# The head of a fused attention and MLP kernel: no entry barrier, eight warm matmuls instead of ten, one copy moved from VectorE to ScalarE

## The chip, the cores and the metric

The kernel runs on one core of one Trainium2 chip. The metric is the device time of one execution in microseconds (us), here the median of several runs. Each run also has a span, from the first to the last of the program's own instructions, which is 1.2 to 1.4 us shorter than the time in most runs. The granted clock is the share of TensorE's full clock that the profile records. PE is TensorE, DVE is VectorE, ACT is ScalarE, POOL is GpSimd, SP is SyncE.

## The reference

The input x has 2048 tokens of 448 values (bfloat16). It is layer-normalised and goes through two branches: a linear attention with 16 heads, and an MLP with squared ReLU. The result is `x + attention * silu(mlp)`.

```python
xn = _layernorm(x, axis=-1)
s = _A_ref(xn, A_wqkv, A_wo)                       # linear attention, then @ wo
g = _silu(_B_ref(xn, B_w1, B_b1, B_w2, B_b2))      # relu(xn @ w1 + b1)**2 @ w2 + b2
return x + s * g
```

Only the first 10 us matter here. In them the first four tiles of 128 tokens are loaded, normalised, transposed on PE, copied from PSUM to SBUF and multiplied with the first weights.

## The kernel before

The kernel records every operation with what it reads and writes. A list scheduler fixes the order on each engine, and each engine then runs its list strictly in order, with semaphore waits. The parts that the change touches (cuts are marked):

```python
# loads: which queue issues them, and in what order
table = add("act", lambda e, _: e.preload_act_table_set("natural_log_exp_and_others"), [], ["actw"], 0.1)
table.prio = -120
load_x(0, 1)                                        # x of tile 0, SP's queue
load_x(1, 2, "act", ["ones"]).prio = -118           # x of tile 1, ACT's queue, after POOL's memset of "ones"
twins = load_k("sp", w_qkv, A_wqkv, "wk", 384, 2 * D, later=True)   # key weights, SP's queue
load_x(2, 4)
# ... (cut)
# layer norm of a tile: statistics on DVE (bn_stats, bn_aggr), Ln and Exp on ACT, normalise on DVE
# ... (cut)
def warm(n, wide=False, after=()):                  # matmuls on constant data
    # ... (cut)
warm(10, wide=True)
# ... (cut)
# the order of the head on DVE and ACT, fixed by hand
("dve", "st0 mv0 st1 mv1 xn00 xn01 xd0 xn10 xn11 xd1 st2 mv2 xT11 st3 mv3 xn2 xd2 xn3 xd3 xT3"),
("act", "ln0 ex0 ln1 ex1 xT00 xT01 xT10 ln2 ex2 b1 ln3 ex3 xT2"),
```

The digit after a name is the tile: `st` and `mv` are its statistics, `ln` and `ex` Ln and Exp, `xn` the normalise, `xd` a small copy beside it, `xT` the copy of the transposed tile out of PSUM. Nothing uses the results of the warm matmuls; they keep PE busy until the first real work. In the profile of this kernel matmuls of 512 columns start 0.427 us apart until about 6.7 us (the slow rate) and 0.216 us apart afterwards (the fast rate).

## Time and profile before

| | before |
|---|---|
| time, median of the first 3 runs | 142.06 us (142.0 to 142.11) |
| span of the profiled run (another one, of 142.56 us) | 141.3 us |
| PE busy | 137.9 us, 98% of the span |
| matmuls back to back from | 9.86 us to the end |
| first transposes on PE | 5.06 us |

These are lines of the page of the kernel before: the busy times with the share of the span, and the chain of work that ended last, followed back from the end.

```profile
PE 137.9 (98%) x1225; PEld 68.3 (48%) x1225; DVE 92.2 (65%) x224; ACT 78.6 (56%) x152; POOL 22.9 (16%) x38
...
PE 98%; DVE 0%; issue 0%; DVEq 0%
```

The kernel is bound by PE. After 9.86 us PE has work without a break, so whatever moves the end has to move the start of this dense stretch, or put a stall into it.

The next lines are from the timeline of the kernel before: its first 7.4 us, and the line with which the dense stretch begins. The columns are start and duration in us, engine, line, operation, what is written from what, and how many; in brackets stands the idle time of the engine before it and what ended it. A DMA line shows the issue alone, not the transfer.

```profile
0.80 0.39 SPq L396 DMA_DIRECT2D x_tok<-in_A_x_dram  x1
...
0.84 4.42 PE L1042 MATMUL pb<-const-bfloat16-1.0 128*128 128x512 bf16 x10 [0.84 <-PEq L1210]
...
0.93 0.40 ACTq L396 DMA_DIRECT2D x_tok<-in_A_x_dram  x1
...
1.25 0.42 SPq L396 DMA_DIRECT2D w_qkv<-in_A_wqkv_dram  x1
...
3.17 0.63 DVE L458 BATCH_NORM_STATS2 st<-x_tok 128x6 f32<-128x448 bf16 x1 [3.17 <-DMA x_tok<-in_A_x_dram]
...
3.93 0.59 DVE L458 BATCH_NORM_STATS2 st<-x_tok 128x6 f32<-128x448 bf16 x1
...
4.66 0.55 DVE L481 TENSOR_SCALAR xn<-x_tok,mv,rstd 128x256 bf16<-128x256 bf16 x2
...
5.06 1.08 PE L510 MATMUL pb<-ident,xn 128*128 128x128 bf16 x6
...
9.86 0.39 PE L621 MATMUL pb<-w_qkv,xT 64*128 64x512 bf16 x2
```

No DMA and no matmul starts before 0.80, because all engines wait for the entry barrier; only POOL's four memsets of constants come earlier, from 0.30.

### The profile page before, as it was taken

How to read it: one execution, taken by the hardware profiler on the slowest of the kernel's cores; microseconds unless marked ns; L12 is line 12 of the kernel's file. 1: busy time of each engine (PE TensorE's matmuls, PEld its weight loads, DVE VectorE, ACT ScalarE, POOL GpSimd, SP SyncE). 2: the span in 40 equal slices, each digit the busy share in tenths (PEclk: the TensorE clock that was granted, in tenths of full speed). 3: DMA queues.
4: the chain of work that ended last, by engine and by line, in shares of the span. 5: the costliest groups of instructions: out<-in, count | busy, mean ns of one | idle time of the engine just before them, and what ended most of it. 6: DMA issues, size and time to landing. Idle time of an engine off the chain costs nothing.

```text
span 141.3 us, 3056 instructions
## 1 busy us (share of the span) xinstructions
PE 137.9 (98%) x1225; PEld 68.3 (48%) x1225; DVE 92.2 (65%) x224; ACT 78.6 (56%) x152; POOL 22.9 (16%) x38
## 2 busy tenths in 40 slices
PE   7999999999999999999999999999999999999992
PEld 2366444444444444444455445644555555555482
DVE  1989978898878997779959910226956062452753
ACT  3658787987888897879799561333033030300220
POOL 6000000000000000000670000000001419092670
DMA  4989266999813400000000026991000202122032
GB/s 117 296 288 264 52 167 115 365 300 195 140 24 70 84 14 0 0 15 8 0 0 0 5 80 148 180 167 21 5 0 0 69 1 89 41 67 68 32 100 69
DMA packets 20210, 12.91 MB, mean 91 GB/s; under 512 B 9380, under 2 KB 19812, under 8 KB 20196
## 3 DMA queue, kind: packets, MB, share of 16 engines
q1 hardware_dynamic: 18188, 11.45, 32.9%
q10 hardware_dynamic: 2008, 1.27, 4.2%
q8 instruction: 10, 0.16, 0.5%
q14 instruction: 4, 0.03, 0.1%
HBM read 8.78 MB, written 2.10 MB: 77 GB/s over the span
## 4 chain that ended last, share of the span: by engine, by line
PE 98%; DVE 0%; issue 0%; DVEq 0%
PE pb L935 30%; PE pb L668 30%; PE pb L621 9%; PE pb L1001 8%; PE pb L702 7%; PE pb L652 6%; PE pb L1042 3%; PE pb L510 1%; PE pb L708 1%; PE pb L795 1%; PE pb L756 1%; PE pb L833 0%; DVE xn L971 0%; PE pb L826 0%; DVE xn L980 0%; PE pb L791 0%
## 5 line engine op out<-in xcount | busy, mean ns | idle before, releaser
L668 PE MATMUL pb<-xT,w 64*128 64x512 bf16 (+2 forms) x408 | 51.3, 365 | 0.0
L935 PE MATMUL pb<-w,r 64*128 64x448 bf16 (+3 forms) x378 | 44.9, 343 | 0.0
L677 ACT ACTIVATE r<-pb,b1f 128x512 bf16<-128x512 f32 x56 | 34.9, 689 | 2.8 <-PE pb L668 2.8
L668 PEld LDWEIGHTS pb<-xT,w 64*128 64x128 bf16 (+1 forms) x408 | 22.8, 94 | 22.1 <-ACT r L677 0.5
L935 PEld LDWEIGHTS pb<-w,r 64*128 64x128 bf16 (+1 forms) x378 | 22.7, 95 | 20.3 <-issue 0.7
L911 ACT ACTIVATE gbuf<-gbuf 128x448 bf16<-128x448 bf16 (+1 forms) x16 | 8.6, 564 | 36.7 <-DVE gbuf L946 34.5
L946 DVE TENSOR_TENSOR gbuf<-pb,b2b 128x448 bf16<-128x448 f32 (+1 forms) x16 | 9.3, 608 | 28.9 <-PE pb L935 28.9
L980 POOL TENSOR_TENSOR xn<-xn,x_tok 128x448 bf16<-128x448 bf16 x15 | 15.0, 1031 | 48.9 <-DVE xn L971 48.9
L621 PE MATMUL pb<-w_qkv,xT 64*128 64x512 bf16 (+1 forms) x106 | 18.0, 380 | 0.0
L652 PE MATMUL pb<-xT,w_qkv 64*128 64x512 bf16 x84 | 15.5, 376 | 0.0
L685 DVE TENSOR_TENSOR r<-r 128x512 bf16<-128x512 bf16 x39 | 13.5, 418 | 0.0
L385 POOL MEMSET kvm<- 128x2048 bf16 x1 | 1.8, 1804 | 64.3 <-DVE zb L646 64.3
L458 DVE BATCH_NORM_STATS2 st<-x_tok 128x6 f32<-128x448 bf16 x16 | 9.3, 612 | 3.6 <-DMA x_tok<-in_A_x_dram 3.6
L609 DVE SCALAR_TENSOR_TENSOR qk<-pb,qk 128x512 bf16<-128x512 f32 x16 | 10.7, 686 | 0.3
L599 ACT ACTIVATE qk<-pb 128x512 bf16<-128x512 f32 x16 | 8.9, 595 | 3.6 <-PE pb L621 3.0
L1001 PE MATMUL pb<-msb,pqT 64*128 64x448 bf16 (+3 forms) x93 | 10.9, 343 | 0.0
L971 DVE TENSOR_TENSOR xn<-pb,gbuf 128x448 bf16<-128x448 f32 (+2 forms) x17 | 9.2, 591 | 2.0 <-ACT gbuf L911 1.5
L686 ACT ACTIVATE r<-r 128x512 bf16<-128x512 bf16 x17 | 9.7, 650 | 0.0
L621 PEld LDWEIGHTS pb<-w_qkv,xT 64*128 64x128 bf16 (+1 forms) x106 | 6.6, 94 | 6.2 <-DVE xT L520 0.2
L702 PE MATMUL pb<-qk,xn 128*128 128x448 bf16 x48 | 9.4, 352 | 0.0
L599 ACT ACTIVATE pqT<-pb 128x512 bf16<-128x512 f32 x12 | 6.8, 597 | 3.2 <-PE pb L668 1.6
L652 PEld LDWEIGHTS pb<-xT,w_qkv 64*128 64x128 bf16 x84 | 6.0, 94 | 5.0
(77 smaller groups left out, 98.9 us busy)
## 6 DMA issues: line engine op xcount, KB each, us to landing
out_dram<-xn SPq DMA_DIRECT2D x15, 112.0 KB, 1.7
w<-in_B_w_dram SPq DMA_DIRECT2D x1, 1568.0 KB, 9.9
x_tok<-in_A_x_dram SPq DMA_DIRECT2D x3, 448.0 KB, 3.8
xT<-rows ACTq DMA_DIRECT2D x6, 112.0 KB
w<-in_B_w_dram SPq DMA_DIRECT2D x1, 576.0 KB, 5.6
xT<-rows SPq DMA_DIRECT2D x5, 112.0 KB
w_o<-in_A_wo_dram SPq DMA_DIRECT2D x1, 392.0 KB, 11.2
w_qkv<-in_A_wqkv_dram SPq DMA_DIRECT2D x1, 384.0 KB, 3.4
```

Of the source, the lines that this page charges most:

```text
L599: add("act", lambda e, _: e.activation(out=slot, in_=src(), func=AF.Exp), [buf, "actw"], [tile], 0.6)
L609: lambda e, _: e.scalar_tensor_tensor(out=slot, in0=src(), scalar=1.0 + 1e-6, in1=slot, op0=ALU.add, op1=ALU.max),
L621: return e.matmul(ps(b)[:, 0:512], xT[half[h], c, si * P : (si + 1) * P], w_qkv[half[h], c, 384 : 2 * D], start=start, stop=stop,)
L652: return e.matmul(ps(b)[:, 0:512], w_qkv[half[h], c, m * P : (m + 1) * P], xT[half[h], c, g * 512 : (g + 1) * 512], start=start, stop=stop,)
L668: return e.matmul(ps(b)[:, c0 : c0 + n], w_1[half[h], c, fi * P : (fi + 1) * P], xT[half[h], c, t : t + n], start=start, stop=stop,)
L677: lambda e, _: e.activation(out=slot, in_=ps(b)[:, 0:512], func=AF.Relu, bias=b1f[:, fi : fi + 1]),
L685: return e.tensor_tensor(out=slot, in0=slot, in1=slot, op=ALU.mult)
L686: return e.activation(out=slot, in_=slot, func=AF.Square)
L702: last = e.matmul(ps(b)[:, 0:D], xn[:, si, c * P : (c + 1) * P], pk_of(si), start=(si == 0), stop=(si == NT - 1),)
L935: return e.matmul(ps(b)[:, 0:n], r2[half[h], fi, si * P : (si + 1) * P], w_2[half[h], fi, c], start=start, stop=stop)
L980: eng, lambda e, _: e.tensor_tensor(out=ob, in0=ob, in1=x_tok[:, si, c], op=ALU.add),
L1001: return e.matmul(ps(b)[:, 0:n], q, m, start=start, stop=stop)
```

## The change

The intent is to start earlier. The entry instructions that the program builder (Bacc) puts in front of the kernel (a drain and a barrier on each engine, four memsets of constants) are filtered out. The warm matmuls, which read one of those constants, now read the kernel's own `ones`, a constant that POOL writes first. There are eight of them, since PE starts earlier. ACT instead of DVE copies the second half of tile 1's transpose, so that DVE can take tile 3's statistics at once. And the load of tile 1 on ACT's queue, which waited for `ones`, now waits for `eps5`, POOL's second memset.

```diff
+    entry = nc.main_func.blocks[0].instructions
+    entry[:] = [i for i in entry if i.opcode not in ("Drain", "EventSemaphore", "Memset")]
 ... (cut)
-        pool(lambda e, _: e.memset(b1r[:, :], 0.0), ["b1r"], dur=0.2)
-        junk = nc.const_aps.tensor(1.0, [P, 512], bf)
+        junk = bass.AP(tensor=ones[:, :].tensor, offset=ones[:, :].offset, ap=[ones[:, :].ap[0], [0, 512]])
+        pool(lambda e, _: e.memset(ones[:, :], 1.0), ["ones"], dur=0.1).prio = -130
+        pool(lambda e, _: e.memset(eps5[:, :], 1e-5), ["eps5"], dur=0.1).prio = -129
+        pool(lambda e, _: e.memset(b1r[:, :], 0.0), ["b1r"], dur=0.2).prio = -128
 ... (cut: the old memsets of eps5 and ones go)
-        load_x(1, 2, "act", ["ones"]).prio = -118
+        load_x(1, 2, "act", ["eps5"]).prio = -118
 ... (cut)
-            add("pe", f, list(after), [b], n * (0.426 if wide else 0.107))
-        warm(10, wide=True)
+            add("pe", f, ["ones", *after], [b], n * (0.426 if wide else 0.107))
+        warm(8, wide=True)
 ... (cut)
-        turn(1, 1, "dve")
+        turn(1, 1, "act")
 ... (cut)
-            ("dve", "st0 mv0 st1 mv1 xn00 xn01 xd0 xn10 xn11 xd1 st2 mv2 xT11 st3 mv3 xn2 xd2 xn3 xd3 xT3"),
-            ("act", "ln0 ex0 ln1 ex1 xT00 xT01 xT10 ln2 ex2 b1 ln3 ex3 xT2"),
+            ("dve", "st0 mv0 st1 mv1 xn00 xn01 xd0 xn10 xn11 xd1 st2 mv2 st3 mv3 xn2 xd2 xn3 xd3 xT3"),
+            ("act", "ln0 ex0 ln1 ex1 xT00 xT01 xT10 xT11 ln2 ex2 b1 ln3 ex3 xT2"),
```

More of the change, by code (lines that the diff above doesn't have):

```diff
@@ L356, in bass_recurrent_scan__linear_attn_block__dense_activation_squared_relu__prompt_kernel @@
         )
-        pool(lambda e, _: e.memset(eps5[:, :], 1e-5), ["eps5"], dur=0.1)
         def keep(name, view, pattern, base, cm):
@@ L373, in bass_recurrent_scan__linear_attn_block__dense_activation_squared_relu__prompt_kernel @@
         pool(lambda e, _: e.memset(eps6[:, :], 1e-6), ["eps6"], dur=0.1)
-        pool(lambda e, _: e.memset(ones[:, :], 1.0), ["ones"], dur=0.1)
         qk_of = lambda si: qk[:, si // 2, :].rearrange("p (j t c) -> p t j c", t=2, c=64)[:, si % 2]
```

## The prediction

> **What bounds it now.** The page gives PE 137.9 of a 141.3 us span, and the chain that ended last is PE for 98% of it. From 9.86 us to the end the timeline shows matmuls back to back. So the end time is the moment at which the dense stretch begins (9.86 us) plus a nearly fixed 131.4 us.
>
> The head, from the timeline: entry barrier until 0.73 us; first x load issued 0.80, statistics of tile 0 start 3.17 when it lands; ten warm matmuls 0.84 to 5.06, 0.427 us apart; first transposes at 5.06, released by DVE's normalised tile at 5.03, so the warm matmuls end just as their successor becomes ready. DVE is then busy 80 to 97% to 9 us. Matmuls run at the slow rate until about 6.70 (starts 0.427 us apart), then 0.216 us apart.
>
> **What the change does.**
> 1. Entry barrier gone. SP ran its drain at 0.0, so x of tile 0 can be issued at about 0.05 instead of 0.80: the whole DVE chain (statistics, normalise, transposes) moves up about 0.7 us. POOL's first memset stays at 0.30, so PE, which needs "ones", starts near 0.47, only 0.37 us earlier.
> 2. Eight warm matmuls: 0.47 + 8 x 0.427 = 3.9; the transposes are ready at about 4.3. PE idles some 0.4 us.
> 3. Clock. The fast rate came 5.9 us after the first matmul. The Trainium skill, "TensorE: Matmul & The Clock Gate", Part 1, says the window is about 3.4 us and free-running; the 5.9 us fits one partly filled window and a full one. If the switch moves with PE's start (0.37 us) or stays, 0.35 to 0.75 us of the first key matmuls run at half rate: 0.2 to 0.35 us of the 0.7 handed back.
> 4. xT of tile 1, second half, to ACT. DVE loses a 0.29 us copy and 0.16 us of wait, so tile 3 statistics start about 0.46 us earlier. But ACT does the copy (0.35 us) before the Ln/Exp of tile 2, which were at 6.93 and 7.25 while PE's transposes for this copy ended near 7.0: rstd of tile 2 comes about 0.45 later and tile 2's normalise hardly moves (8.02 before, relative to the chain). Tile 3's Ln stands behind the b1 copy on ACT, which waits for PE, so its normalise (8.70) does not move either. Worth 0 to 0.1 us.
>
> Sum: 0.7 - 0.2 (clock) + 0.05, about 0.55 us at the start of the dense stretch, all on the critical path, since PE is dense afterwards. The list schedule is recomputed; I allow 0.2 us either way for rearranged evictions later.
>
> **Predicted: 141.5 us, range 141.05 to 141.95.** Faster by over 2%: 0.01; within 2%: 0.98; slower: 0.01.
>
> **What would show it.** First x issue at 0.0 to 0.1 and first statistics near 2.4 to 2.5; first warm matmul 0.4 to 0.5, the eighth over by 3.9; a gap of PE of about 0.4 us; first transposes near 4.3; the fast rate from 6.3 to 6.7 at latest, so that the first key matmuls show 0.427 us; DVE idle about 0.4 us before tile 2's normalise; dense stretch from about 9.3; from there to the end still 131.4 us.
>
> **What would make it wrong.** The switch could come one window earlier or later: up to 0.5 us either way. The first load could take longer when issued this early. The later schedule could gain or lose stalls. The clock that times the kernel could start later than the first instruction, hiding part of the 0.7 us.

## The result, and the profile after

The changed kernel takes 144.28 us (median of 6 runs, 143.67 to 146.08) against 142.09 us before (6 runs): it is slower, by 1.4%. That is inside the band of 2% to which the prediction gave 0.98, but outside its range and on the other side. The ratio is 1.0139, with a 95% interval of 1.0112 to 1.0167. A ratio is the mean time of one kernel's fast runs over that of the other's of the same rounds, so it is not quite the ratio of the medians. The run of 146.08 us counts as slow (over 1.5% above the fastest) and is not in it. The runs of the changed kernel also scatter more.

Here is the timeline of the changed kernel over the same 7.4 us, and the start of its dense stretch (its line numbers are higher by one):

```profile
0.00 0.40 SPq L397 DMA_DIRECT2D x_tok<-in_A_x_dram  x1
...
0.45 3.38 PE L1043 MATMUL pb<-ones 128*128 128x512 bf16 x8 [0.45 <-POOL eps L351]
0.45 0.42 SPq L397 DMA_DIRECT2D w_qkv<-in_A_wqkv_dram  x1
0.46 0.42 ACTq L397 DMA_DIRECT2D x_tok<-in_A_x_dram  x1
...
2.15 0.63 DVE L459 BATCH_NORM_STATS2 st<-x_tok 128x6 f32<-128x448 bf16 x1 [2.15 <-DMA x_tok<-in_A_x_dram]
...
4.32 0.63 DVE L459 BATCH_NORM_STATS2 st<-x_tok 128x6 f32<-128x448 bf16 x1 [1.32 <-DMA x_tok<-in_A_x_dram]
...
5.08 0.55 DVE L482 TENSOR_SCALAR xn<-x_tok,mv,rstd 128x256 bf16<-128x256 bf16 x2
...
5.45 1.00 PE L511 MATMUL pb<-ident,xn 128*128 128x128 bf16 x6 [1.62 <-DVE xn L482]
...
11.28 0.39 PE L622 MATMUL pb<-w_qkv,xT 64*128 64x512 bf16 x2
```

The first two things went as hoped. The load of tile 0 goes out at 0.00 and its statistics start at 2.15 instead of 3.17, a full microsecond earlier. Then comes the surprise: DVE sits idle for 1.32 us, waiting for x of tile 1. It was issued at 0.46, earlier than before by 0.47 us, and yet it lands later. Since `st1` stands ahead of `xn00` in DVE's list, the finished statistics of tile 0 wait too, and PE gets its first transposes at 5.45 instead of 5.06, after 1.62 us of idleness. The chain of waits of the changed kernel, in order of time over its first 12 us, says so in one line (start, duration, what): it runs through a DMA of 3.84 us.

```profile
0.11 0.35 ACT L435
0.46 3.84 DMA x_tok<-in_A_x_dram
4.30 0.02 issue
4.32 0.64 DVE st L459
```

The order of the two issues explains where to look. Before, tile 1 went out 0.32 us ahead of the key weights. Now the barrier no longer lines SP and ACT up: SP starts at 0.00, while ACT's load waits for POOL's memset. So the key weights go out at 0.45 and tile 1 at 0.46. The page's list of DMA issues (KB, and us from issue to landing) shows that the key weights became slower as well; first the kernel before,

```profile
w_qkv<-in_A_wqkv_dram SPq DMA_DIRECT2D x1, 384.0 KB, 3.4
```

then the changed kernel:

```profile
w_qkv<-in_A_wqkv_dram SPq DMA_DIRECT2D x1, 384.0 KB, 4.2
```

The second loss is the clock. This is a table by stretch of the changed kernel: us, busy us of PE, PEld (the weight loads of PE), DVE, ACT and POOL (with the number of instructions), the granted PE clock, the share of the DMA engines and GB/s.

```profile
0.00:3.50 3.50, 3.05 (x8) 1.04 (x8) 0.81 (x2) 1.72 (x3) 2.40 (x13) 1.00 0.60 140
3.50:6.90 3.40, 1.75 (x13) 0.78 (x11) 2.48 (x9) 1.64 (x6) 0.00 (x0) 1.00 1.13 297
6.90:10.30 3.40, 3.40 (x18) 2.03 (x16) 2.11 (x8) 1.38 (x6) 0.00 (x0) 0.50 1.02 342
```

The last of these stretches in the kernel before:

```profile
6.90:10.30 3.40, 3.40 (x34) 2.07 (x32) 2.69 (x9) 1.76 (x7) 0.00 (x0) 1.00 0.90 277
```

From 3.5 to 6.9 us PE is busy for only 1.75 of 3.40 us, and in the next stretch the granted clock is 0.50. This is where half of its first six key matmuls and its first six MLP matmuls stand: it gets through 18 matmuls, against 34 in the same stretch before. The matmuls bear the record out: key matmuls start 0.427 us apart there. The trace's marks of the clock lie 3.413 us apart (at 3.485, 6.898 and 10.311 us). The time from the first transposes to the dense stretch grows from 4.80 us (5.06 to 9.86) to 5.83 us (5.45 to 11.28).

This is the profiled run. Of the six runs only this one and one other have a recorded clock of 0.988, which is what such a half window makes of the mean; the other four have 1.000 and took as long (143.67 to 146.08 us). A record of 1.000 doesn't rule out slow matmuls, since the kernel before has it too, with the slow rate until about 6.7 us. How those four runs lost their time is not seen.

The books of the two profiled runs (142.56 and 144.38 us; the first is 0.5 us above its kernel's median, so their difference is less than the 2.19 us between the medians): the dense stretch starts 1.42 us later (0.39 of it before the transposes, 1.03 after them). Another 0.24 us is a stall near 100 us, where PE waits for an eviction of DVE that stands behind DVE's wait for a load of replicated denominators. This stall is in 6 of the 13 profiles of this document and varies: the gap between two matmul starts there, about 0.19 us when nothing waits, was 0.35 before and 0.59 after. Together that is 1.66 us, against 1.64 us of growth of the span (141.31 to 142.95).

### The profile page after: what moved, and what is told of

Read it like the earlier page. It is cut to its first block, busy times and chain, and to the rows that moved or that the text cites. A ratio compares the mean times of both kernels' runs of the same rounds, so it can differ in the third digit from the quotient of the medians.

```text
span 143.0 us, 3037 instructions
## 1 busy us (share of the span) xinstructions
PE 138.1 (97%) x1223; PEld 68.9 (48%) x1223; DVE 91.9 (64%) x223; ACT 79.0 (55%) x153; POOL 22.7 (16%) x34
## 4 chain that ended last, share of the span: by engine, by line
PE 87%; DMA 8%; DVE 2%; ACTq 1%; issue 1%; ACT 0%; DVEq 0%
PE pb L669 30%; PE pb L936 24%; PE pb L622 9%; PE pb L1002 8%; PE pb L703 6%; PE pb L653 6%; DMA xT<-tiles 5%; DMA x_tok<-in_A_x_dram 3%; PE pb L511 1%; PE pb L709 1%; ACTq L397 1%; PE pb L834 0%; DVE st L459 0%; DVE gbuf L947 0%; DVE xn L972 0%
## 5 line engine op out<-in xcount | busy, mean ns | idle before, releaser
L669 PE MATMUL pb<-xT,w 64*128 64x512 bf16 (+2 forms) x408 | 52.0, 367 | 0.0
L622 PE MATMUL pb<-w_qkv,xT 64*128 64x512 bf16 (+1 forms) x106 | 18.5, 385 | 0.0
```

What stands on the lines that cost most here:

```text
L622: return e.matmul(ps(b)[:, 0:512], xT[half[h], c, si * P : (si + 1) * P], w_qkv[half[h], c, 384 : 2 * D], start=start, stop=stop,)
L669: return e.matmul(ps(b)[:, c0 : c0 + n], w_1[half[h], c, fi * P : (fi + 1) * P], xT[half[h], c, t : t + n], start=start, stop=stop,)
```

## The experiments

**Theory A.** Tile 1 is late because its load goes out together with the key weights instead of ahead of them; DVE's fixed order passes the delay on to tile 0; and the idle PE then loses its clock, which makes a small delay a large one. **Rival B.** Loads issued this early, or without the barrier, are slow by themselves. **Rival C.** Eight warm matmuls are too few, whatever the loads do. **Rival D.** The copy moved to ACT is the fault.

All runs below gave correct results. Except where it is said, only the edit differs. By the 2% class all rows are "same", except b_x1_behind, which is "unclear" since its interval holds 1.02; what is compared below is the intervals.

| kernel | median us (range) | before, same rounds | ratio, 95% interval |
|---|---|---|---|
| the change | 144.28 (143.67 to 146.08) | 142.09 | 1.0139 (1.0112 to 1.0167) |
| a_x1_free | 141.67 (141.14 to 142.5) | 142.18 | 0.9964 (0.9933 to 0.9995) |
| a_wk_later | 142.03 (141.72 to 142.7) | 142.28 | 0.9990 (0.9964 to 1.0015) |
| b_x1_late (edit had no effect) | 142.13 (142.05 to 142.22) | 142.18 | 0.9988 (0.9969 to 1.0007) |
| b_x1_behind | 144.88 (143.71 to 145.82) | 142.28 | 1.0181 (1.0138 to 1.0223) |
| a_warm12 | 142.51 (142.07 to 143.29) | 142.18 | 1.0019 (0.9992 to 1.0046) |
| a_warm10 | 142.56 (142.09 to 143.06) | 142.28 | 1.0020 (0.9994 to 1.0046) |
| b_no_barrier | 142.65 (142.38 to 143.57) | 142.18 | 1.0035 (1.0005 to 1.0065) |
| b_warm8 | 142.61 (142.29 to 144.46) | 142.28 | 1.0027 (0.9999 to 1.0055) |
| b_xT_act | 142.13 (141.85 to 142.75) | 142.21 | 0.9998 (0.9975 to 1.0022) |
| a_x1_free_warm9 | 141.66 (141.17 to 142.32) | 142.21 | 0.9953 (0.9927 to 0.9978) |
| nb_x1_free_warm9 | 141.64 (141.31 to 141.77) | 142.21 | 0.9949 (0.9932 to 0.9967) |

Names with a_ start from the changed kernel, those with b_ and nb_ undo or do parts as told.

### a_x1_free: the changed kernel, tile 1's load first and without a wait

```diff
-        load_x(1, 2, "act", ["eps5"]).prio = -118
+        load_x(1, 2, "act").prio = -121
```

> The changed kernel; its one edit: the load of x tile 1 waits for nothing and stands first on ScalarE's queue (issue near 0.1 us instead of 0.46, so ahead of the 576 KB key weights issued at 0.45). Theory A (tile 1 lands late, 4.30 us, because the key weights got onto the DMA engines first, and DVE's in-order statistics of tile 1 hold up everything): tile 1 lands before 3.0, first transposes at or before 4.5 instead of 5.45, dense stretch from about 9.4 to 9.9, time 141.2 to 142.0. Theory B (loads issued this early are slow whatever their order): tile 1 still lands near 4.0 or later, time within 0.5 us of 144.3. Theory C (eight warm matmuls are too few and the clock is taken back): the gap before the transposes shrinks but stays, so the clock is still halved for 3.4 us in some runs and the time stays above 143.

(The key weights' load is 384 KB, as the page has it; the 576 KB in this expectation is a slip.)

Measured: 141.67 us, 2.6 us less than the changed kernel and 0.5 less than before. The timeline of its first microseconds:

```profile
0.00 0.39 SPq L397 DMA_DIRECT2D x_tok<-in_A_x_dram  x1
...
0.12 0.40 ACTq L397 DMA_DIRECT2D x_tok<-in_A_x_dram  x1
...
0.44 0.42 SPq L397 DMA_DIRECT2D w_qkv<-in_A_wqkv_dram  x1
...
3.10 0.59 DVE L459 BATCH_NORM_STATS2 st<-x_tok 128x6 f32<-128x448 bf16 x1
...
4.20 1.00 PE L511 MATMUL pb<-ident,xn 128*128 128x128 bf16 x6 [0.15 <-DVE xn L482]
```

Tile 1 goes out 0.32 us ahead of the key weights and lands at 2.56 us. DVE no longer waits for it, the transposes start at 4.20, the dense stretch at 8.73 (earlier than the 9.4 to 9.9 expected). After the fast rate was granted, at 4.71 us, there is no half clock in the span, though there are still eight warm matmuls. This one edit takes the whole loss away. Rivals B and C had it stay, and D would have too.

### a_wk_later: the changed kernel, the key weights issued later

```diff
-        twins = load_k("sp", w_qkv, A_wqkv, "wk", 384, 2 * D, later=True)
+        twins = load_k("sp", w_qkv, A_wqkv, "wk", 384, 2 * D, reads=["ident"], later=True)
```

> The changed kernel; its one edit: the key weights' load on SyncE waits for POOL's ident (near 1.24 us) and so goes out near 1.28 instead of 0.45; the load of x tile 1 keeps its wait and its issue at 0.46. Theory A (tile 1 is late because the key weights are in flight beside it, not because of its own issue time or of the missing barrier): tile 1 lands before 3.0 (2.5 us of flight as in the kernel before, not 3.84), first transposes at 4.1 to 4.5, time 141.2 to 142.3. Rival B (a load issued this early is slow by itself, or the hold behind POOL's memset is the fault): it lands near 4 and the time stays above 143.5.

Measured: 142.03 us. From its timeline:

```profile
0.46 0.40 ACTq L397 DMA_DIRECT2D x_tok<-in_A_x_dram  x1
...
1.26 0.40 SPq L397 DMA_DIRECT2D w_qkv<-in_A_wqkv_dram  x1
...
3.90 1.00 PE L511 MATMUL pb<-ident,xn 128*128 128x128 bf16 x6
```

Tile 1's load was issued at 0.46, exactly as in the changed kernel, and landed at 2.51 instead of 4.30. Its wait behind POOL's memset did no harm by itself; what did was the company of the key weights, or of the loads behind them on SP's queue, which go out later here too (x of tiles 2 and 3 at 1.71 instead of 0.92); the packets below b_x1_behind speak for the key weights. The transposes started at 3.90. The dense stretch did not start earlier than in the last run (8.84), because now the key weights (landed 4.84) and x of tiles 2 and 3 (landed 5.49) were late: DVE waited 0.50 us for the latter. A load moved back has to be paid for by somebody. That is not why the median is 0.36 us above that of a_x1_free, though: the spans are as short (140.33 us on the mean, against 140.30), and the difference lies outside them (see "What stays open").

### b_x1_late: a control that failed

```diff
-        load_x(1, 2, "act", ["ones"]).prio = -118
+        load_x(1, 2, "act", ["eps6"]).prio = -118
```

> The kernel before, with barrier, ten warm matmuls and the old copies; its one edit: the load of x tile 1 waits for a later memset of POOL, so that it is issued near 1.28 us, together with the key weights at 1.25, as in the changed kernel, instead of at 0.93. Theory A: tile 1 lands near 5.0 instead of before 3.9, DVE's second statistics start there, first transposes near 6.1 instead of 5.06, time 143.0 to 144.5. Theories B and C: nothing of theirs is in this kernel, so at most the 0.35 us by which the issue was moved, 142.1 to 142.5.

Measured: 142.13 us against 142.18. It says nothing about A. The scheduler saw that a load now needs `eps6` and moved that memset to the front of POOL's list, so the load still went out at 0.93, landing at 3.42. The run is of use as a second copy of the kernel before: at the same instruction order and another phase of the clock (fast from 5.63 us) its dense stretch started at 9.54 instead of 9.86.

### b_x1_behind: the kernel before, tile 1 issued behind the key weights

```diff
-        load_x(1, 2, "act", ["ones"]).prio = -118
+        load_x(1, 2, "act", ["ident"]).prio = -118
```

> The control that the run with POOL's later memset failed to be (there the memset was only moved first, and the issue stayed at 0.93). The kernel before, barrier and ten warm matmuls in place; the load of x tile 1 waits for the finished ident, issue near 1.6 us, behind the key weights at 1.25 instead of ahead of them at 0.93. Theory A: its flight grows from 2.50 to 3.5 us or more, it lands at 5.0 or later, first transposes at 6.0 or later, time 142.9 to 144.5. If only the later issue counts (0.65 us, flight unchanged): it lands near 4.1, DVE's second statistics come 0.2 us later than now, time 142.2 to 142.5.

Measured: 144.88 us, a loss of 2.6 us on the kernel with its barrier, its ten warm matmuls and its old copies. (POOL's other early memsets come after `ident` here; the chain of waits does not pass through them.) The two issues in its timeline, and its chain of waits:

```profile
1.26 0.42 SPq L396 DMA_DIRECT2D w_qkv<-in_A_wqkv_dram  x1
...
1.56 0.43 ACTq L396 DMA_DIRECT2D x_tok<-in_A_x_dram  x1
```

```profile
1.56 3.63 DMA x_tok<-in_A_x_dram
5.20 0.02 issue
5.22 0.64 DVE st L458
```

The issue is 0.63 us later than before, the landing 1.77 us later (5.20 instead of 3.43), PE then idles for 1.68 us, and the trace has the clock at half from 7.35 to 10.77 us. So the damage of the change can be made without any other part of it, by the order of two loads. Rival B is out: here the barrier is in place, and in a_x1_free and a_wk_later tile 1 flew fast without it.

The flights of the two loads from issue to landing, in the profiled runs, worked out from the marks of the landings:

| kernel | tile 1 issued, relative to the key weights | tile 1, us | key weights, us |
|---|---|---|---|
| a_wk_later | 0.80 ahead | 2.05 | 3.58 |
| before | 0.32 ahead | 2.50 | 3.38 |
| a_x1_free | 0.32 ahead | 2.44 | 3.42 |
| the change | 0.01 behind | 3.84 | 4.24 |
| b_x1_behind | 0.30 behind | 3.63 | 3.51 |

A third of a microsecond of lead decides 1.3 us of flight. The other eight profiles agree: with a lead of 0.32 or 0.33 us tile 1 took 2.49 to 2.56 us, and issued within 0.02 us behind the key weights 3.60 to 4.17 us. The trace's DMA packets show the company directly (tile 1 has 128 of 896 bytes on ACT's queue, the key weights 384 of 1024 bytes on SP's). Before, tile 1's packets started within 0.74 us, the first ahead of all the key weights', and 42 of these had started when its last one did. In the change they were spread over 1.78 us, with 26 of the key weights' packets ahead of the first and 355 ahead of the last. In b_x1_behind 314 were ahead of the first.

The Trainium skill, "DMA: Bandwidth & Descriptors", section "Issuing engines are not separate DMA queues", says that DMAs of several engines run on the same 16 DMA engines and interleave, which agrees with the late tile. The section does not say that two loads issued in the same instant are both slower. Here they were: in the change, the key weights were issued 0.80 us earlier than before and landed at 4.69 us, against 4.63. Why that is so was not settled by these runs.

### a_warm12 and a_warm10: the changed kernel with more warm matmuls

```diff
-        warm(8, wide=True)
+        warm(12, wide=True)      # a_warm12;  warm(10, wide=True) in a_warm10
```

> The changed kernel with twelve warm matmuls, not eight: they end near 5.6 at the slow rate, so TensorE hardly idles before the transposes at 5.45, while tile 1 stays late. Splits the loss in two. If the clock being taken back (the profile has it at half from 6.90 to 10.31) is the larger part (C): no stretch at half clock, matmuls of the first keys 0.216 us apart, time 142.3 to 142.8 and runs much closer together. If lateness of tile 1 is nearly all (A alone): 143.5 or more. The sum of the parts that I work out from the profiles: tile 1 about 0.4 us, clock about 1.0 us of the 1.42 us by which the dense stretch is later.

> The changed kernel with ten warm matmuls instead of eight, nothing else: late tile 1 and the copy on ScalarE stay. Together with the entry part alone (142.65, ten warm, copy on DVE) and the changed kernel (144.28, eight warm, copy on ScalarE) this splits those 1.6 us. If the count of warm matmuls is the cause, by way of the clock (idle time before the transposes 0.75 instead of 1.6 us): 142.3 to 142.9. If the copy on ScalarE with the moved statistics is the cause: 143.8 or more.

Measured: 142.51 and 142.56 us. Two more warm matmuls, with tile 1 still late (landed at 4.06 in the profile of a_warm10, at 4.63 in that of a_warm12), win back 1.7 of the 2.2 us. The table by stretch of a_warm10:

```profile
0.00:3.50 3.50, 3.05 (x8) 1.13 (x9) 0.81 (x2) 1.75 (x3) 2.40 (x13) 1.00 0.60 159
3.50:6.90 3.40, 2.84 (x16) 1.19 (x15) 2.68 (x10) 1.71 (x7) 0.00 (x0) 1.00 1.07 290
6.90:10.30 3.40, 3.40 (x37) 2.14 (x37) 2.87 (x10) 2.23 (x8) 0.00 (x0) 1.00 1.04 330
```

PE is busy 2.84 instead of 1.75 us between 3.5 and 6.9, the clock stays at 1.00, and 37 instead of 18 matmuls fit into the stretch after it. So most of the loss went through the clock. The rest, 142.56 against 141.66 us for a_x1_free_warm9 below, is lateness: in the profiles the transposes start 0.95 us apart and the dense stretches 0.93 us.

Twelve matmuls did not fill the gap, contrary to what I had expected: in the profile of a_warm12 (143.29 us, the slowest of its runs) they come at the fast rate from about 4 us on and are over at 4.96, and PE idles for 0.83 us until the transposes at 5.79. That did not cost it the clock.

My expectation of a split, 0.4 us for tile 1 and 1.0 for the clock, was read from one profile and does not carry over to the time: the clock's part is 1.5 to 1.7 us (of the 1.72 us between the dense stretches of the two profiles, 0.24 us lie before the transposes).

### b_no_barrier: the entry part of the change alone

As an edit of the changed kernel:

```diff
-        warm(8, wide=True)
+        warm(10, wide=True)
-        turn(1, 1, "act")
+        turn(1, 1, "dve")
 ... (and the two lists of the head as before)
```

Against the kernel before, the built program differs in the entry instructions, POOL's memsets and the source of the warm matmuls.

> Of the change, the entry part alone: barrier and constants gone, x tile 1 waiting for POOL's second memset as in the changed kernel, but ten warm matmuls and the copy of tile 1 on DVE as before. Theory A: tile 1 lands near 4.3 as in the changed kernel, transposes near 5.4; with ten warm matmuls until 4.7 TensorE idles 0.7 instead of 1.6 us, so the clock is less often taken back: 142.3 to 144. If the copy on ScalarE were the fault, this kernel would be at 141.5 or so; if eight matmuls were the only fault, likewise at 141.5 to 142.

Measured: 142.65 us. Taking the barrier out does not gain; it costs 0.5 us, since tile 1 is late here as well (issued 0.46, landed 4.34, transposes 5.50).

### b_warm8: the kernel before with eight warm matmuls

```diff
-        warm(10, wide=True)
+        warm(8, wide=True)
```

> The kernel before with eight warm matmuls, nothing else. They end near 4.25, the transposes come at 5.03 as before: 0.8 us of idle TensorE. If eight are harmful by themselves: the clock is taken back or comes later in some runs, median 142.5 to 143.5 and a wide spread. If eight hurt only together with the late tile 1 (idle of 1.6 us): 142.0 to 142.3 as the kernel before.

Measured: 142.61 us, not clear of 142.28 (the interval reaches 0.9999), but with two runs at 143.47 and 144.46 us. The profile fell on the run of 144.46, which counts as slow. In it the key matmuls are 0.427 us apart until 8.76 us, 2.1 us longer than in the profile of before, and the gap between two matmul starts at DVE's eviction near 100 us is 1.31 us. That explains this slow run alone. Whether eight do harm by themselves, as rival C has it, the fast runs (142.29 to 143.47) leave open; it is at most a small part of what is lost.

### b_xT_act: the copy on ACT and the moved statistics alone

As an edit of the kernel before:

```diff
-        turn(1, 1, "dve")
+        turn(1, 1, "act")
 ... (and the two lists of the head as in the change)
```

> Of the change, the last part alone: the second half of tile 1 is copied by ScalarE and tile 3's statistics move up on DVE; barrier, ten warm matmuls and loads as before. If this part is harmless, as the profiles say (from tile 2's statistics to the dense stretch 3.52 us with the copy on DVE and 3.32 with it on ScalarE, where the clock was fast): 141.8 to 142.1, a gain of 0 to 0.3. If it carries some of the 2.2 us lost: 142.5 or more.

Measured: 142.13 us against 142.21. Rival D is out. The profiled runs agree with a small gain in the head (dense stretch from 9.42, against 9.54 in the twin of the kernel before), which the time does not show.

### a_x1_free_warm9 and nb_x1_free_warm9: the version that the experiments point to

Both are the changed kernel with tile 1's load first and without a wait, and nine warm matmuls. The second has the copy of tile 1 back on DVE, with the old lists.

```diff
-        load_x(1, 2, "act", ["eps5"]).prio = -118
+        load_x(1, 2, "act").prio = -121
-        warm(8, wide=True)
+        warm(9, wide=True)
```

> The candidate that should beat both kernels: the changed kernel with the load of x tile 1 first on ScalarE's queue and waiting for nothing, and nine warm matmuls, which end near 4.29 us, where the transposes become ready (4.20). Theory A with the clock as its amplifier: tile 1 lands near 2.6, transposes 4.2 to 4.4, dense stretch 8.7 to 8.9, no half clock, time 141.1 to 141.7, runs closer together than with eight. If something else holds this kernel back: 141.9 or more.

> The same candidate with the copy of tile 1 back on DVE and the statistics of tile 3 behind it. The difference to the candidate is what the last part is worth once the loads are right: 0.2 us slower by the profiles (dense stretch near 9.0), 141.3 to 141.9. If the copy on ScalarE is a burden: faster than the candidate.

Measured: 141.66 and 141.64 us, both faster than the kernel before by 0.5%, with intervals clear of 1. In the profile of a_x1_free_warm9 the ninth warm matmul gives way to the transposes at 4.26 us without a gap:

```profile
0.45 4.02 PE L1043 MATMUL pb<-ones 128*128 128x512 bf16 x9 [0.45 <-POOL eps L351]
...
4.26 0.98 PE L511 MATMUL pb<-ident,xn 128*128 128x128 bf16 x6
```

The dense stretch starts at 8.63 us, 1.2 earlier than in the profile of before. The runs are hardly closer together than with eight matmuls and the early load (a range of 1.15 us against 1.36), and the median is the same (on another chip), so the ninth matmul is not shown to help. The copy's place makes no difference to the time: the 0.2 us that I expected are not there.

### What stays open

The span of a_x1_free_warm9 is 140.27 us on the mean of its runs, that of nb_x1_free_warm9 140.22. The time does not follow in full. In the 30 runs of b_x1_late, b_warm8, b_xT_act and the last 12 of the kernel before, the time exceeds the span by 1.19 to 1.30 us. In the 48 runs without the barrier it does so by 1.22 to 2.5 us, in 12 of them by over 1.45 (b_x1_behind, with the barrier, has two such runs as well). So a part of what is won inside the span is lost outside it in some runs. No view of the profile shows where.

## Why the prediction was wrong

The prediction was 141.5 us, in a range of 141.05 to 141.95, and the kernel took 144.28.

- **The step that failed** is the first: "the whole DVE chain (statistics, normalise, transposes) moves up about 0.7 us". It was worked out from the load of tile 0 alone. That load did move up, by 0.80 us, and its statistics by 1.02 us (I had 2.4 to 2.5 us, measured 2.15). But the chain has a second input. Tile 1's load moved up by only 0.47 us, the key weights by 0.80, so the two met and tile 1 landed 0.87 us later than before. I had noted when each engine would start and had not compared the starts of two loads with each other. a_x1_free, a_wk_later and b_x1_behind show this cause from both sides.
- **"PE idles some 0.4 us"** followed from it and became 1.62 us.
- **The clock term had the wrong event.** I put it at 0.2 to 0.35 us, for a switch to the fast rate that comes late, and the risk of a switch one window off at 0.5 us. What came in the profiled run was another thing: the fast rate was granted early, at 3.485 us, and taken back at 6.898 us. Filling the idle time with two more warm matmuls recovers 1.7 us. The reason given in the prediction, that the window is free-running (the Trainium skill, "TensorE: Matmul & The Clock Gate", Part 1), agrees with the traces: the marks are 3.413 us apart and the switch came 5.86 us after the first matmul before (by the spacing of its matmuls), 3.04 us in the change and 4.26 us in a_x1_free.
- **"Worth 0 to 0.1 us"** for the copy on ACT fits: 142.13 against 142.21 and 141.66 against 141.64, no effect clear of the noise.
- **The dense stretch** was taken to keep its 131.4 us from the first matmul to the end of the span. It took 131.7 in the profile; the 0.24 us are the stall near 100 us, within the 0.2 us or so that the prediction allowed for.
- **The gain itself was real, only not in this kernel.** With tile 1's load ahead of the key weights, the change gives 141.67 us, and 141.66 with nine warm matmuls: near the 141.5 that I had written for the change as it stood. That is partly luck: the dense stretch began at 8.73 us and not at the 9.3 forecast, and part of what this won did not reach the time.

## What to carry to other kernels

A barrier at entry also lines the engines up (here the first instructions of SP, ACT, POOL and PE behind it came at 0.79 to 0.84 us, and without it at 0.00 to 0.45 us). When it goes, compare the issue times of all early loads with one another, above all of a small load that starts the critical chain on one queue and a large one on another: keep the small one ahead by some tenths of a microsecond. When a fixed in-order list puts the second tile's work before the first tile's result, the later of two loads sets the start. And do not cut warm matmuls to fit the best case: while the first real work can be late, the price of idle PE time can be a window at half clock, as after 1.62 us here.

## What the Trainium skill lacked or had wrong

- "TensorE: Matmul & The Clock Gate", the table of the two states in Part 1, by which the clock falls after an idle window of about 3.4 us, and the advice against idle gaps of over about 3 us: here a gap of 1.62 us inside one window, with PE busy 1.75 of 3.40 us (transposes counted as busy), was followed by a window at half clock, and so was one of 1.68 us in b_x1_behind. A whole idle window was not needed. Gaps of 0.83 us (a_warm12), 0.60 us (b_no_barrier) and 0.54 us (a_warm10) did not have this effect in the profiled runs.
- The same page calls the trace's clock events unreliable; that agrees. The page of the kernel before has no clock row at all, while its matmuls were 0.427 us apart until about 6.7 us and 0.216 us afterwards. The spacing of matmuls was the safer sign.
- "DMA: Bandwidth & Descriptors" says that DMAs of several engines interleave, but gives no figure for what a small lead of one over another is worth. Here 112 KB took 3.84 us beside 384 KB issued 0.01 us earlier, and 2.50 us when issued 0.32 us ahead; the large load took 4.24 and 3.38 us.
- "Runtime: NRT & Kernel Launch" counts launch costs outside the kernel, but no page has the cost of a program's own entry barrier: 0.80 us here until the first load went out. In some runs without it, up to 1.2 us more than usual lay outside the span, for no reason that the profile shows.
